# Segment 0 of an attention and Fourier kernel: x turned on the matrix engine, every q and k projected into padded rows, a Fourier token stage in 64-row tiles

## The chip, the cores and the metric

The kernel is one program on one core of a Trainium2 chip. A core has five engines with an instruction stream each: TensorE (PE in the profile, its weight loads PEld), VectorE (DVE), ScalarE (ACT), GpSimd (POOL) and SyncE (SP). SP computes nothing here; it issues nearly all DMAs. Matrix products go to PSUM, eight banks of 128 partitions x 512 f32. The metric is the device time of one execution in microseconds (us).

## The reference

x is 2048 tokens x 640 channels in bf16. Two branches read it, and a gate for each token mixes them.

```python
# branch A: 32 heads of 20 channels, 4 segments of 512 tokens
phi = lambda t: where(t > 0, t + 1, exp(t))
for s in range(4):
    p = softmax(qs @ ks.T * 20**-0.5 + causal_mask)   # inside the segment
    a_dot = p @ vs
    a_mem = (phi(qs) @ M) / (phi(qs) @ z + 1e-6)      # memory of earlier segments
    out[s] = sigmoid(beta) * a_mem + (1 - sigmoid(beta)) * a_dot
    M += phi(ks).T @ vs;  z += phi(ks).sum(tokens)
a = concat(out) @ wo
# branch B: a filter in frequency space, w_r and w_i are 2048 x 321
b = irfft2(rfft2(x) * (w_r + 1j * w_i))
g = sigmoid((x * gate_w).sum(-1));  result = g * a + (1 - g) * b
```

Segment 0 reads no memory, so its q needs no phi; segment 3 updates none, so its k needs none.

## The kernel before

**How the order is set.** Every step is recorded first: a function for each engine that can run it, and the buffers it reads and writes. Which engine takes a step, and the order on each engine, come from one long written list, `ORDER`: each number names an operation and one of its engines. Semaphore waits follow from the buffers. Engines run strictly in their order, so a waiting instruction holds back all behind it on its engine; a DMA that waits on SP holds back the later DMAs on SP. PSUM banks 0 to 3 form one unit, for the scores of four heads at a time; banks 4 to 7 are handed out singly to all other products. PSUM is copied out ("evicted") by ACT (line L523) or DVE (L525).

**Segment 0's start.** Ten matmuls on zeros (`NWARM`) keep PE busy until data arrives. x comes transposed (channels on partitions, tile `xT`) by three transposing DMAs on SP (L546). wq and wk come in two parts, the first 192 columns first.

**q and k.** A head has 20 rows, and a product for the scores wants each head at a partition that is a multiple of 32: the padded tiles `qkp`. For the first two head groups of segment 0 (a group is 4 heads) `proj_direct` (L961) makes these rows on PE directly, four 32-column tiles at a time, which run side by side. All else goes through `proj_tile` (L1027): 128 packed channels per product, evicted to `qu` (for segment 0 to `q0`), stored to DRAM (`qk_scr`, L548) and loaded back with the padding (`pad`, `pad2`, L548). `proj_tile` also makes phi for each 128-channel tile: an exponential on ACT (L1072), a max-add and a min on DVE (L1084, L1085). phi of k then goes through transposing DMAs (`pkT`, L546) into `pkn`, tokens on partitions, for the memory update (`mem_update`, L1334).

**Scores and outputs.** `qk_unit` (L1227) computes the scores of four heads in 12 matmuls of 20 x 64 weights, eight running side by side; ACT takes exp of up to 2048 columns in one instruction (L1263), GpSimd masks the diagonal blocks (L1284). `pv_group` multiplies by v and scales (L1320 to L1330). `mem_read` and `denominators` (L1202 to L1213) build the memory's part: its reciprocals `rc` go to DRAM (`r_scr`) and come back spread over rows (`r`), `finish_tile` (L1506) multiplies (L1526) and adds (L1534), and the output projection (L512) follows.

**Fourier branch** (`fft`, L1365), woven in between. F1 transforms 16 residues of the tokens with the matrix `fcat` (folds at L901, L906); its result goes to `Ac`. For each of 16 groups of token frequencies: D transforms along channels into two tiles `Bt` (real and imaginary); T, four matmuls of 128 x 128 weights and 321 columns, turns tokens and gives two PSUM banks; one DVE product per bank with the filter (`W_mul`, L1439, 642 columns) gives four products `Pt`; two additions on DVE or GpSimd (`W_add`, L1444) give `Yt`; Tb, six matmuls of 256 columns, turns tokens back, into `Cp`. The tables for T and Tb come by DMA (`tt`, 512 KB for two groups), the filter by 32 loads `Wt`. At the end Cp is transformed back along channels and joined with the gate into `G` (L1485).

Of the kernel before, what the change touches and what calls it, by code (L numbers as in the profile page):

```python
# [10 lines left out]
F32 = dt.float32  # L11
# [38 lines left out]
class Sched:  # L50
# [58 lines left out]
    COST = {(0, 1): 94.0, (0, 2): 94.0, (1, 0): 110.0, (1, 2): 110.0, (2, 0): 110.0, (2, 1): 94.0}  # L109

    def schedule(self, pools, order, nsem=56):
# [14 lines left out]
        for i, o in enumerate(pe):  # L126
            o.emode = o.mode
            if o.mode < 0:
                modes = [held[id(b)] for b in o.banks if id(b) in held]
                if not modes and i and pe[i - 1].emode != 1:  # L130
                    modes = [pe[i - 1].emode]
                for q in pe[i + 1:] if not modes else ():
                    m = q.mode if q.mode >= 0 else held.get(id(q.banks[0]), -1)
                    if m >= 0:
                        modes = [0 if m == 1 else m]
                        break
                o.emode = (modes + [0])[0]
            if o.emode != 1:
                for b in o.banks:
                    held[id(b)] = o.emode  # L140
# [167 lines left out]
def make_tables():  # L308
# [42 lines left out]
    T = np.zeros((16, 128, 4, 128))  # L351
    Tp = np.zeros((16, 128, 2, 2, 16, 4, 2))
    n2 = np.arange(16)
    k2 = np.arange(16)
    for g in range(16):
        for half in range(2):
            for i in range(4):
                kb, pi_, kind, sg = pair_of(g, half, i)
                k = kb + 128 * k2
                ph = 2 * pi * np.outer(n2, k) / S  # L360
                c, s = np.cos(ph), np.sin(ph)
                m = half * 64 + k2 * 4 + i
                kr = n2 * 8 + pi_ * 2
                ki = kr + 1

                def put(t, rows, val):
                    T[g, rows[:, None], t, m[None, :]] = val
                if kind == "pair":
                    put(0, kr, c), put(0, ki, sg * s), put(1, kr, -s), put(1, ki, sg * c)
                    put(2, kr, -s), put(2, ki, sg * c), put(3, kr, -c), put(3, ki, -sg * s)  # L370
                else:
                    src = kr if kind == "zero" else ki
                    put(0, src, c), put(1, src, -s), put(2, src, -s), put(3, src, -c)

                def putp(r, typ, eo, val):
                    for q in range(16):
                        Tp[g, m[q], r, typ, :, pi_, eo] = val[:, q]
                if kind == "pair":
                    putp(0, 0, 0, c), putp(1, 0, 0, -s), putp(0, 0, 1, -sg * s), putp(1, 0, 1, -sg * c)
                    putp(0, 1, 0, -s), putp(1, 1, 0, -c), putp(0, 1, 1, -sg * c), putp(1, 1, 1, sg * s)  # L380
                else:
# [1225 lines left out]
```

## Time and profile before

| what | value |
|---|---|
| time, median of 3 runs (lowest, highest) | 243.88 us (243.15, 245.06) |
| span of the profiled execution | 245.4 us |
| instructions | 10243 |
| PE busy | 228.8 us, 93% |
| ACT busy | 199.9 us, 81% |
| DVE busy | 195.6 us, 80% |
| POOL busy | 166.4 us, 68% |
| DMA engines, mean share of queue 1 | 69.2%, 40.96 MB |

The profile is one execution. Its busy table gives each engine's time at work; the slices divide the span into 40 equal parts of 6.1 us and show in tenths how busy each engine was, the clock granted to PE (9 is full) and the share of the DMA engines. Groups of instructions are listed by line and tile with mean times; windows give the same busy times for a chosen stretch. The profiled span lies 1.5 us above the median of the runs, so a change is worked out in microseconds against the span and then taken from the median.

### The profile page before, as it was taken

The page shows a single profiled execution, that of the slowest core. Times are in us where ns is not written, and L with a number is a line of the kernel's source. Part 1 is how long each engine was busy: PE and PEld are TensorE (multiplying, and loading weights), DVE is VectorE, ACT ScalarE, POOL GpSimd, SP SyncE. Part 2 cuts the span into 40 slices and gives each one's busy share as a digit, 9 for nine tenths or more (in the row PEclk, how much of TensorE's full clock was granted, in tenths as well). Part 3 has the DMA queues.
Part 4 walks back from the last instruction along what each step waited for, and adds up shares of the span by engine and source line. Part 5 has one row for each costly group of instructions (what it writes and reads, how often), then busy time and mean ns, then how long its engine had stood idle before and what let it go on. Part 6 is the DMA issues. An engine that isn't in the chain of part 4 may idle for free.

```text
span 245.4 us, 10243 instructions
## 1 busy us (share of the span) xinstructions
PE 228.8 (93%) x4347; PEld 140.8 (57%) x4361; DVE 195.6 (80%) x481; ACT 199.9 (81%) x241; POOL 166.4 (68%) x297
## 2 busy tenths in 40 slices
PE   7899999999999999999899999899999997699994
PEld 2574567765455665545556555465454565366794
DVE  0479998889999987989999898989889867435563
ACT  2289698988999999999899889999999976388740
POOL 8513268557969846768947998859898694359730
PEclk9999999999999999999999999999999999589999
DMA  7999959975799875575698661375758997812123
GB/s 168 278 365 208 239 160 178 318 140 164 210 200 174 168 226 143 125 199 135 202 233 234 185 186 53 99 210 146 222 151 194 230 140 96 127 36 85 57 84 108
DMA packets 58928, 42.17 MB, mean 172 GB/s; under 512 B 30020, under 2 KB 55172, under 8 KB 58884
## 3 DMA queue, kind: packets, MB, share of 16 engines
q1 hardware_dynamic: 57844, 40.96, 69.2%
q8 instruction: 34, 0.56, 1.0%
q10 hardware_dynamic: 1040, 0.57, 0.8%
q14 instruction: 10, 0.08, 0.1%
HBM read 23.32 MB, written 12.30 MB: 145 GB/s over the span
## 4 chain that ended last, share of the span: by engine, by line
PE 54%; DVE 18%; ACT 12%; DMA 10%; issue 3%; SPq 1%; DVEq 0%
PE psum L514 48%; ACT ex L1263 9%; PE psum L512 6%; DMA pkn<-phk 4%; DMA r_scr<-rc 3%; DMA xT<-in_A_x_dram 2%; DVE xsb L906 2%; DVE Pt L1439 2%; DVE xf L901 1%; DVE phk L1085 1%; ACT et L1072 1%; DVE oU L1526 1%; DVE G L1485 1%; DVE ub L525 1%; DVE va L1115 1%
## 5 line engine op out<-in xcount | busy, mean ns | idle before, releaser
L1263 ACT ACTIVATE ex<-psum 128x2048 bf16<-128x2048 f32 (+4 forms) x92 | 138.7, 1507 | 16.3 <-PE psum L514 14.3
L1284 POOL TENSOR_SCALAR_AFFINE_SELECT ex<-ex 128x256 bf16<-128x256 bf16 (+2 forms) x224 | 122.1, 567 | 42.0 <-ACT ex L1263 38.4
L514 PE MATMUL psum<-qkp 20*64 20x64 bf16 (+5 forms) x1280 | 32.7, 271 | 4.8 <-issue 2.3
L514 PE MATMUL psum<-xT,wk 128*128 128x256 bf16 (+1 forms) x280 | 34.0, 273 | 0.9 <-DMA wk<-in_A_wk_dram 0.6
L514 PE MATMUL psum<-wv,xT 128*32 128x321 bf16 (+3 forms) x400 | 30.0, 301 | 0.6 <-DVE va L1115 0.3
L514 PE MATMUL psum<-xT,wq 128*128 128x512 bf16 (+1 forms) x121 | 27.0, 380 | 1.3 <-DMA xT<-in_A_x_dram 0.7
L1439 DVE TENSOR_TENSOR Pt<-psum,Wt 128x642 bf16<-128x642 f32 x32 | 25.5, 820 | 2.3 <-PE psum L514 1.9
L514 PEld LDWEIGHTS psum<-qkp 20*64 20x64 bf16 x1280 | 13.4, 103 | 19.5 <-ACT ex L1263 13.2
L514 PEld LDWEIGHTS psum<-xT,wk 128*128 128x128 bf16 (+1 forms) x280 | 19.9, 97 | 7.0 <-DMA wk<-in_A_wk_dram 1.1
L512 PE MATMUL psum<-wo,oU 128*32 128x320 bf16 x480 | 23.4, 313 | 0.5 <-DVE oU L1534 0.5
L906 POOL TENSOR_TENSOR xsb<-xf 128x320 bf16<-128x320 bf16 (+2 forms) x12 | 9.2, 763 | 17.1 <-DVE xsb L906 13.2
L525 DVE CAST ot<-psum 128x320 bf16<-128x320 f32 x21 | 10.1, 491 | 12.9 <-PE psum L512 10.5
L514 PEld LDWEIGHTS psum<-wv,xT 128*32 128x32 bf16 (+1 forms) x400 | 14.3, 96 | 8.3 <-issue 2.4
L514 PE MATMUL psum<-big,Ac 128*128 128x160 bf16 (+2 forms) x96 | 18.1, 258 | 0.7 <-DVE Pt L1439 0.3
L1115 DVE TENSOR_TENSOR va<-psum,ebx 128x320 bf16<-128x320 f32 x32 | 15.2, 483 | 4.2 <-ACT gate L1113 2.1
L514 PE MATMUL psum<-big,Cp 128*128 128x321 bf16 (+1 forms) x96 | 18.0, 302 | 0.2 <-DVE G L1485 0.2
L514 PE MATMUL psum<-ex,va 128*32 128x64 bf16 (+3 forms) x576 | 17.4, 256 | 0.7 <-DVE dn L1152 0.3
L1485 DVE TENSOR_TENSOR G<-eo,psum 128x320 bf16<-128x320 f32 x32 | 14.7, 482 | 3.9 <-PE psum L514 2.8
L512 PEld LDWEIGHTS psum<-wo,oU 128*32 128x32 bf16 x480 | 12.4, 100 | 8.8 <-issue 4.2
L514 PE MATMUL psum<-tt,Yt 128*128 128x256 bf16 (+1 forms) x96 | 16.5, 275 | 0.3
L514 PEld LDWEIGHTS psum<-ex,va 128*32 128x32 bf16 x576 | 11.1, 96 | 9.7 <-POOL ex L1284 3.4
L1072 ACT ACTIVATE et<-qu 128x512 bf16<-128x512 bf16 x25 | 15.6, 630 | 0.2
(99 smaller groups left out, 391.9 us busy)
## 6 DMA issues: line engine op xcount, KB each, us to landing
qkp<-qk_scr SPq DMA_DIRECT2D x28, 160.0 KB
tt<-tab_tt SPq DMA_DIRECT2D x8, 512.0 KB, 4.3
qk_scr<-qu SPq DMA_DIRECT2D x12, 256.0 KB, 3.1
u_scr<-ub SPq DMA_DIRECT2D x12, 256.0 KB, 3.9
xsb<-in_A_x_dram SPq DMA_DIRECT2D x8, 320.0 KB, 6.8
oU<-u_scr SPq DMA_DIRECT2D x15, 128.0 KB, 2.9
out_dram<-ot SPq DMA_DIRECT2D x12, 160.0 KB
Wt<-in_B_w_r_dram SPq DMA_DIRECT2D x16, 80.2 KB, 2.6
```

Of the source, the lines that this page charges most:

```text
L512: h = e.matmul(dst, wt, r_, start=st, stop=sp_, **{**kw, "tile_position": (0, q), "skip_group_check": True})
L514: h = e.matmul(o_, l_, r_, start=st, stop=sp_, **kw)
L525: alts["dve"] = (lambda e: e.tensor_copy(dst(), src()), 67 + 1.04 * n, 68.0)
L901: self.either(lambda e, r=r, op=op: e.tensor_tensor(xf.ap(r * 642, [321, 2], [1, 320]), xs.ap(o, [D, 2], [1, 320]), xs.ap(o + 320, [D, 2], ...
L906: self.either(lambda e, dst=dst, src=src, d0=d0, n=n, op=op: e.tensor_tensor(xs.ap(o + dst, [D, 2], [1, n]), xf.ap(src + d0, [321, 2], [1, ...
L1072: self.one("act", lambda e: e.activation(et.ap(0, [1, L]), qsl(), ACT.Exp), L, [qb], [b("et", pi_)], late, name="phi_exp")
L1085: fmin = lambda e: e.tensor_tensor(dst(), dst(), et.ap(0, [1, L]), ALU.min)
L1115: self.one("dve", lambda e: e.tensor_tensor(va.ap(i * H * VW + h0 * VW, [VW, nh], [1, DH]), self.ps(bank, 0, [DH, nh], [1, DH]), self.ebx. ...
L1263: self.one("act", lambda e, d=d, q=q: e.activation(self.ex.ap(*d), self.ps(bank, *q), ACT.Exp, scale=SC), n, [bank], [self.exb(s, 2 * pr + ...
L1284: self.one("pool", lambda e: e.affine_select(self.ex.ap(e0 + d0, [1280, 4], [1, n], np_=np_), self.ex.ap(e0 + s0, [1280, 4], [1, n], np_=np_),
L1439: self.one("dve", lambda e, ri=ri, Pt=Pt, Wt=Wt, wo_=wo_, bank=bank: e.tensor_tensor(Pt.ap(ri * 322, [644, 2], [1, KD]), self.ps(bank, 0, ...
L1485: self.one("dve", lambda e, q=q, n2=n2, bank=bank, eo=eo: e.tensor_tensor(self.G.ap(n2 * D + 639 * q, [1 - 2 * q, 320]), eo.ap(q, [1, 320] ...
```

## The change

- **Segment 0's x** is loaded untransposed by two plain DMAs, one on SP and one on ACT's queue, into `xn`, which lies in the third score buffer. `x_turn` turns it on PE: 20 matmuls of 128 columns against the identity in `fcat`, five evictions into `xT`. The zero matmuls go from ten to eight.
- **Segment 0's q and k** all go through `proj_direct`: 16 units instead of 4, each 128 padded rows, straight into `qkp`. The nine packed tiles of segment 0, their stores to DRAM, and the padded loads of segment 0 go.
- **Segment 0's phi of k** comes from `k_tokens`: k is turned token-major on PE (8 banks, 40 matmuls of at most 80 columns), and exp, max and min read or follow these banks, 384 or 256 columns at a time, into `pkn`. Segment 0's three `pkT` transposes go.
- **Fourier token stage**: T's weights are 64 x 128, two row tiles at partitions 0 and 64 with a PSUM bank each (`mode=3`); each bank holds the real and the imaginary part of 64 frequencies. `W_mul` keeps its size and gives `UV`; `W_add` goes, its signs are in Tb's table. Tb has four matmuls of 128 columns per channel block in place of two of 256, writing runs of 4 elements at a stride of 8. The filter is loaded into 64 partitions (36 loads) and copied to the other 64 by 8 DMAs `W_dup` (SP), each waiting for its loads. `tt` is 384 KB.
- **phi of later segments** runs over pairs of tiles: ten instructions of 1024 columns and five of 512 in place of 25 of 512, on each of exp, max and min, with one buffer `et`.
- The gate's transpose runs in 32-column tiles, `rc` lies in `dnc`'s place, and `ORDER` is a new list.

The core of the diff ("..." marks what is left out, all of `ORDER` among it):

```diff
-  NWARM = 10
+  NWARM = 8
...
-  self.xt_load(0, 0.0, 0, 1)
-  self.xt_load(0, 0.01, 1, 2)
-  self.xt_load(0, 0.02, 3, 2)
+  for i in range(2):
+    self.dma(lambda i=i: self.xn.ap(2 * i * D, [D, 2], [1, D]), lambda i=i: dap(x, 2 * i * P * D, [D, P], [P * D, 2], [1, D]),
+        2 * P * D * 2, [], [self.b("xn", i)], 0.0, name="ld_xn")
...
+def x_turn(self):
...
+  for c in range(5):
...
+    bank = Bank(1, "gen", "qk")
+    for i in range(2):
...
+      for q in (2 * i, 2 * i + 1):
+        def th(q=q, c=c, bank=bank):
+          return (self.ps(bank, q * P, [1, P]), self.xn.ap(q * D + c * P, [1, P]), self.fcat.ap(P, [1, P]), True, True, {})
...
+      self.mms(items, [b("xn", i), b("fcat"), bank] + [self.exb(0, 2, k) for k in ("a0", "b0", "b1", "c0", "m1", "m3")], [], -0.9, name="turn", mode=0)
+    self.Sc.op(self.copy_alts(lambda c=c: self.xT[0].ap(c * L, [1, L]), lambda bank=bank: self.ps(bank, 0, [1, L]), L),
...
   else:
-    for n_, (g, which) in enumerate(((0, "q"), (0, "k"), (1, "q"), (1, "k"))):
-      self.proj_direct(which, g, -0.5 + 0.1 * n_, xT, xb)
+    self.x_turn()
+    for n_ in range(16):
+      self.proj_direct("qk"[n_ % 2], n_ // 2, -0.5 + 0.1 * n_, xT, xb)
+    self.k_tokens()
   k = 0
...
+  for half in range(2 if s else 0):
...
-      if s == 0 and half == 0:
...
-          self.dma(lambda j=j, w_=w_, pad=pad: pad.ap((4 * w_ + 2) * L, [L, 2], [1, L], p0=32 * j, np_=DH),
...
-              DH * 2 * L * 2, [b(which + "d", s, half, x) for x in range(2)], [b(which + "p", pidx, j, gl) for gl in (2, 3)], prio, name="pad2")
...
-  pad = self.qkp[0]
+  pad, pidx, gl = self.qkp[g // 4], g // 4, g % 4
+  np_ = 116 if g == 7 else P
+      m = DH if g == 7 and hh == 3 else 32
...
+  self.Sc.op(self.copy_alts(lambda: pad.ap(p0_ + gl * L, [1, L], np_=np_), lambda: self.ps(bank, 0, [1, L], np_=np_), L),
...
+def k_tokens(self):
...
+  for x in range(4):
+    for t0, nt in ((0, 3), (3, 2)):
...
+      bank = Bank(1, "gen")
...
+      for g in range(8):
+        f = max(f0, 80 * g)
+        e_ = min(f1, 80 * g + 80)
...
+        while f < e_:
...
+          def th(g=g, f=f, hh=hh, d=d, n=n, mv=mv, x=x, f0=f0, bank=bank):
+            np_ = 116 if g == 7 else P
+            return (self.ps(bank, f - f0, [1, n]), self.qkp[g // 4].ap((4 + g % 4) * L + x * P, [1, P], np_=np_),
+                self.fcat.ap(P + 32 * hh + d, *mv, np_=np_), True, True, {})
...
+      self.one("act", lambda e, src=src, es=es, m=m: e.activation(self.et.ap(es, [1, m]), src(), ACT.Exp), m, [bank], [eb], 1.0, name="kt_exp")
+      self.one("dve", lambda e, src=src, dst=dst: e.tensor_scalar(dst(), src(), 0.0, 1.0, ALU.max, ALU.add), m, [bank], db, 1.0, name="kt_max")
+      self.Sc.op({"dve": (lambda e, dst=dst, es=es, m=m: e.tensor_tensor(dst(), dst(), self.et.ap(es, [1, m]), ALU.min), 67 + 0.52 * m, 68.0)},
...
+  if t in (1, 2, 4) and ((which == "q" and s >= 1) or (which == "k" and s <= 2)):
+    n = 1 if t == 2 else 2
...
+    et = self.et
-    self.one("act", lambda e: e.activation(et.ap(0, [1, L]), qsl(), ACT.Exp), L, [qb], [b("et", pi_)],
...
+    self.one("act", lambda e: e.activation(et.ap(0, [1, m]), src(), ACT.Exp), m, both, [b("et")], late, after=[b("ets", q) for q in range(2)], fix=94, name="phi_exp")
...
-    self.Sc.op({"dve": (fmax, 67 + 0.26 * L, 68.0)}, r=[qb], w=[db], prio=late, name="phi_max", lock=True, after=alias)
-    self.Sc.op({"dve": (fmin, 67 + 0.52 * L, 68.0)}, r=[b("et", pi_)], w=[db], prio=late, name="phi_min", lock=True)
...
+    self.Sc.op({"dve": (fmax, 67 + 0.26 * m, 68.0)}, r=both, w=db, prio=late, name="phi_max", lock=True)
+    self.Sc.op({"dve": (fmin, 67 + 0.52 * m, 68.0)}, r=[b("et")], w=db, prio=late, name="phi_min", lock=True)
...
-        lambda c=c, nb=nb: self.Ac.ap(c * 2048 + nb * 32, [P, 16], [8, 4], [1, 8]),
...
+        lambda c=c, nb=nb: self.Ac.ap(c * 2048 + nb * 16, [64, 32], [4, 4], [1, 4]),
+        lambda bank=bank: self.ps(bank, 0, [4, 32], [P, 4], [1, 4]), 512),
...
-      self.dma(lambda tt=self.tt[ti]: tt.ap(0, [1024, 2], [1, 1024]), lambda g=g: dap(self.tab["tt"].ap(), g * P * 1024, [1024, P], [P * 1024, 2], [1, 1024]),
...
-          self.dma(lambda r=r, Wt=Wt, h=h, slot=slot, step=step: Wt.ap(r * 644 + slot * KD, [step * KD, 2], [1, KD], p0=64 * h, np_=64),
...
+            self.dma(lambda r=r, Wt=Wt, h=h, o=o, n=n: Wt.ap((4 * r + o) * KD, [KD * 4 // n, n], [1, KD], p0=32 * h, np_=32),
...
+        self.dma(lambda Wt=Wt: Wt.ap(0, [1, 8 * KD], p0=64, np_=64), lambda Wt=Wt: Wt.ap(0, [1, 8 * KD], np_=64), 64 * 8 * KD * 2, wkeys,
+          [b("Wd", wi)], early, name="W_dup")
...
-      self.mms(items, [b("tt", ti), b("Bt", g % 2, 0), b("Bt", g % 2, 1), bank], [], prio2, name="T", mode=0)
-      self.one("dve", lambda e, ri=ri, Pt=Pt, Wt=Wt, wo_=wo_, bank=bank: e.tensor_tensor(
-        Pt.ap(ri * 322, [644, 2], [1, KD]), self.ps(bank, 0, [0, 2], [1, KD]), Wt.ap(wo_, [644, 2], [1, KD]), ALU.mult), 2 * KD,
-        [bank] + wb, [Pb[ri][0], Pb[ri][1]], prio2, after=self.after_q0(("Pt", g % 2, ri)), name="W_mul")
...
-      fn = lambda e, r=r, a0=a0, a1=a1, op=op, Pt=Pt, Yt=Yt: e.tensor_tensor(
-        Yt.ap(r * 322, [1, KD]), Pt.ap(a0 * 322, [1, KD]), Pt.ap(a1 * 322, [1, KD]), op)
-      self.either(fn, KD, [Pb[0][r], Pb[1][1 - r]], [Yb[r]], prio2, after=self.after_q0(("Yt", g % 2, r)), name="W_add")
...
+    UV = self.UV[g % 2]
...
+    pb = [Bank(1, "gen") for _ in range(2)]
...
+    for q in range(2):
+      for rh in range(2):
+        def th(q=q, rh=rh, tt=tt, to=to, Bt=Bt, pb=pb):
+          return (self.ps(pb[rh], 0, [1, KD]), tt.ap(to + q * P, [1, P], p0=64 * rh, np_=64), Bt.ap(q * 322, [1, KD], p0=64 * rh, np_=64),
+              q == 0, q == 1, {"tile_position": (64 * rh, 0)})
...
+    self.mms(items, [b("tt", ti), b("Bt", g % 2, 0), b("Bt", g % 2, 1)] + pb, [], prio2, name="T", mode=3)
+    for rh in range(2):
+      self.one("dve", lambda e, rh=rh, UV=UV, Wt=Wt, gp=gp, bank=pb[rh]: e.tensor_tensor(
+        UV.ap(rh * 644, [322, 2], [1, KD]), self.ps(bank, 0, [0, 2], [1, KD]), Wt.ap((2 * rh + gp) * KD, [4 * KD, 2], [1, KD]), ALU.mult), 2 * KD,
+        [pb[rh]] + wb, [Ub[rh]], prio2, name="W_mul")
...
-            return (self.ps(bank, (c % 2) * 256, [1, 256], np_=kc), Yt.ap(r * 322 + c * P, [1, kc]), tt.ap(to + 512 + r * 256, [1, 256]),
...
-        self.mms(items, Yb + [b("tt", ti), bank], [], prio3, name="Tb", mode=0)
+        for rh in range(2):
+          for w in range(2):
+            def th(c=c, rh=rh, w=w, kc=kc, UV=UV, tt=tt, to=to, bank=bank):
+              return (self.ps(bank, (c % 2) * 256 + rh * 4, [8, 32], [1, 4], np_=kc), UV.ap(rh * 644 + w * 322 + c * P, [1, kc]),
+                  tt.ap(to + 256 + (2 * rh + w) * P, [1, P]), w == 0, w == 1, {"skip_group_check": True})
...
```

## The prediction, on record before the result

> **What bounds the kernel now.** I read the busy table and the slices first, then windows by stage.
>
> ```profile
> PE   7899999999999999999899999899999997699994
> ACT  2289698988999999999899889999999976388740
> DVE  0479998889999987989999898989889867435563
> DMA  7999959975799875575698661375758997812123
> ```
>
> PE is at nine tenths nearly everywhere; ACT and DVE stand at eight or nine until slice 32. No engine is far from full, so an engine that is relieved hands the bound to the next. The windows cut the span at the first exp of the scores (13.30 us) and the first exp of segment 3 (175.50). Columns: stretch, us, busy us of PE, PEld, DVE, ACT, POOL with counts, granted clock, DMA share, GB/s.
>
> ```profile
> 13.00:36.00 23.00, 22.54 (x313) 14.17 (x303) 21.43 (x55) 19.53 (x30) 8.18 (x12) 1.00 0.95 240
> 13.30:175.50 162.20, 156.21 (x2641) 94.71 (x2654) 146.89 (x360) 149.33 (x180) 113.33 (x210) 1.00 0.74 187
> 175.50:245.40 69.90, 62.03 (x1556) 40.62 (x1554) 44.47 (x114) 47.45 (x57) 44.23 (x75) 0.95 0.59 124
> 205.00:209.00 4.00, 3.17 (x108) 2.08 (x106) 3.86 (x12) 2.47 (x4) 1.40 (x1) 1.00 1.00 113
> 211.40:216.20 4.80, 4.79 (x69) 2.43 (x72) 1.39 (x4) 2.74 (x4) 1.50 (x3) 0.50 0.75 117
> ```
>
> In the **middle** (13.30 to 175.50) PE is busy 96.3%, ACT 92.1%, DVE 90.6%. In the **tail** (from 175.50) PE has 7.9 us of gaps, ACT and DVE over 22. Between the last two windows PE stands still for 2.35 us in the middle of a score unit:
>
> ```profile
> 211.41 0.21 PE L514 MATMUL psum<-qkp 20*64 20x64 bf16 x1 [2.35 <-issue]
> ```
>
> "issue" means that nothing in the profile released it: PE had no instruction. One of the 34 instruction fetches (16 KB each, queue 8) was under way while the DMA share was 1.00. Then the clock is halved from 209.4 to 216.2, 6.8 us, which cost about 3.4. Together this **lull** costs 5.75 us.
>
> **The change, part by part.** Prices of PE work come from these rows (start, us, engine, shape, count):
>
> ```profile
> 9.78 1.05 PE L514 MATMUL psum<-xT,wk 128*32 128x256 bf16 x32
> 11.60 1.25 PE L514 MATMUL psum<-xT,wk 128*128 128x256 bf16 x10
> 32.15 0.64 PE L514 MATMUL psum<-fcat,xsb 128*128 128x128 bf16 x8
> 120.41 0.44 PE L514 MATMUL psum<-Bt,tt 128*128 128x321 bf16 x2
> ```
>
> A row lasts one matmul's latency plus a pitch for each further one. Ten matmuls of 256 columns: (1.25 - 0.27) / 9 = 0.109 us. Thirty-two 32-column tiles of 256 columns, four side by side: (1.05 - 0.27) / 7 = 0.111 for four, so a padded unit costs as much as a packed tile, five products of 512 columns, 1.08 us. For 128 columns the pitch is 0.056 to 0.060, for 321 about 0.14.
>
> *PE work.* Segment 0 has 16 padded units in place of 4 units and 9 packed tiles: +3 x 1.08 = +3.3. Turning x: 20 x 0.056 = +1.1. Turning k: 40 matmuls of 80 columns or fewer; at the 128-column pitch 2.4, by columns 1.3; I take 1.3. T: 64 x 0.14 = 9.0 falls to half if the two row tiles run side by side, -4.5; the nearest row is the four 32-column tiles above, which do. Tb: 96 x 0.109 = 10.5 becomes 192 x 0.056 = 10.75, +0.3. Two more switches of tiling than before by the order of instructions, 0.1 each by the gaps at such places, +0.2. Sum **+1.7**, so the change does not relieve PE as a whole. What the trace does not show: whether two row tiles run side by side (bounds -4.5 and 0; no row excludes either), and what Tb's writes in runs of 4 at a stride of 8 cost (no gain, as columns do not fall; at most a doubled pitch, 192 x 0.056 = +10.8). For both I take the nearest rows, whose time follows columns alone.
>
> The Trainium skill ("TensorE: Matmul & The Clock Gate", Measured speedup vs the span model) gives 3.07 times for four row tiles; scaled to two, T would fall by 3.1 instead of 4.5, an estimate, and the forecast would be 1.4 later. No run here shows it yet.
>
> *ACT work.* An exp of 1024 columns takes 1024 ns and one of 512 takes 598, so a pair saves 0.17: 10 pairs of phi, -1.7. Segment 0's phi of k: five of 635 ns become eight of 384 or 256 columns, about 0.49 and 0.38, +0.3. The new list moves evictions (595 ns on ACT, 685 on DVE) to DVE and drops segment 0's: -5 net. Sum **-6 to -7**.
>
> *DVE work.* W_mul stays, 32 of 820 ns. W_add goes: 16 of 370 ns on DVE, -5.9, and 16 of 731 on GpSimd, -11.7. Pairs of phi save about 0.06 on each max and min. The evictions from ACT and the three of x take this back: sum **about 0**. GpSimd takes up other elementwise work, net -6; it is not on the path.
>
> *DMA.* Segment 0 loses three transposing loads of x, 8 stores and 12 padded loads of q and k, and three pkT transposes; one of those stood 4.95 us on the chain of waits (from 71.84). tt moves 1 MB less. Added: four filter loads and 8 copies W_dup, each waiting on SP for its filter loads. Behind a W_dup on SP stand the padded loads and stores of segment 1; SP's waits for filter data are not in the trace of before, and its longest DMA wait (for r_scr) is 3.8 us. Filter loads land in 2.6 us, so a W_dup put right behind them blocks SP at most about that long; where it is put later, nothing. The scores that need those padded loads are released by exps, every 1.9 us, so the cost is 0 to 2.6 for the one that is hit; I take 0, as the next two or three score units are already loaded.
>
> *In time, start.* Before, the first projection waits for x until 5.59 and the first exp starts at 13.31. After, plain loads land like those at the start of the trace: 240 KB issued at 0.80 landed at 4.8, 320 KB issued at 0.79 at 4.1. With 5.3 for both halves of x, 0.3 for the first turns, three evictions on DVE (2.05), the 3.9 of projection that then remain ahead of the first scores and 0.55 for these, the first exp starts at 12.1: **-1.1**. Bounds: -2 if x lands at 4.4; +0.5 if PE idles between the eight zero matmuls and x and the clock halves.
>
> *In time, middle.* I counted the work that stands ahead of segment 3's first exp in both orders, with the trace's mean times: PE -2.3, ACT -6.8, DVE -2. The Fourier groups are spread later, so PE's share moves behind that point. The stretch can shrink by no less than PE's 2.3 if its 6 us of gaps stay, and by ACT's 6.8 if ACT paces it. "ACT ex waits for PE" sums to 14.3 us in 29 waits and "PE waits for ex" to 13.2 in 42: they pace each other about equally, so I take the middle: **-4.5**.
>
> *In time, tail.* PE has 3.8 us more behind that exp and 7.9 us of gaps, 2.35 of them the lull. Bounds 0 and +3.8, half taken: **+1.9**. The lull I leave as it is: the same kind of burst (transposes of the outputs, tables) meets the same code.
>
> Sum: -1.1 - 4.5 + 1.9 = -3.7. Against the profiled execution 245.4 - 3.7 = 241.7; it lay 1.5 above the median, so **243.88 - 3.7 = 240.2**. A change within 1% (241.4 to 246.3) can hardly be told from none by these runs.
>
> **Rivals.**
>
> 1. *The lull goes.* Thirty-three of 34 fetches stop nobody; one falls into a full DMA window. All transfers shift, so it may simply miss: 240.2 - 5.75 = **234.4**.
>
> 2. *DVE holds the middle.* DVE is busy 90.6% there, W_mul is not shorter, and evictions are moved to it. If it takes ACT's place the middle gains nothing: 243.88 - 1.1 + 1.9 = **244.7**, no change. Against it: ACT gives up work that DVE takes only as W_add goes. The Trainium skill ("TensorEngine Tiling (Array Packing)", PSUM Bottleneck) warns of this: tiling speeds up TensorE, but not the emptying of PSUM. The rows agree that W_mul's share stays; by this rule T's saving would be worth nothing in the middle.
>
> 3. *PE runs out of instructions in segment 0* (slower). The 16 padded units are 480 matmuls and 480 weight loads in 17 us of PE time, 55 instructions per us; in 205 to 209, ahead of the lull, it was (108 + 106) / 4 = 53, and the DMA share was 1.00 there and is 0.95 in 13 to 36. From 210 to 232 PE ran as fast at a share of 0.38 without a stop. So both conditions meet in the new segment 0, unless the DMAs that go (the q, k round trip) empty the queues. Each stall costs up to 5.75: one gives 245.9, two **251.7**; it decides from the second on.
>
> 4. *The change doesn't do what it says*: row tiles one after the other give 240.2 + 4.5 = 244.7, Tb at twice its pitch 240.2 + 10.8 = **251**.
>
> **How the numbers follow.** Forecast 0.44, with its own range 237.2 to 243.2 (middle and tail at their bounds, start aside); lull gone 0.20; DVE 0.17; instruction supply 0.13; not as said 0.06. Faster by over 1%: three quarters of the forecast 0.33, the lull 0.20, DVE 0.01, together 0.54. Within 1%: 0.11 + 0.11 + 0.03 = 0.25. Slower: DVE 0.05, supply 0.10, not as said 0.06, together 0.21. The range is 234 to 249: it leaves out about half of the lull's case below and the dearest cases above.
>
> **What the profile after would show.** Right: the first exp near 12.1; T's row with four matmuls of 321 columns in the time of two; no L1444 and 32 W_mul of some 820 ns; ACT's sum down by 6; the first exp of segment 3 near 170. Wrong: the filter product waiting behind evictions with DVE over 95% busy; "issue" waits above 1 us before 30 us and a clock of 0.5 after them; Tb's 128-column rows at 0.1 apart; SP waiting for filter loads while PE waits for qkp. What would upset the forecast most is a lull that goes, comes twice, or comes elsewhere.

## The result, and the profile after

| | median of runs, us (lowest to highest) | profiled execution: span, time | ratio to before |
|---|---|---|---|
| before, beside it | 244.47 (243.15 to 246.54, 4 runs) | 245.4, – | 1 |
| after | 256.99 (253.21 to 259.4, 4 runs) | 256.6, 258.44 | 1.045, 95% interval 1.034 to 1.056 |

The change costs about 4.5%; the ratio is taken over the faster executions of each kernel, the medians over all four, and the profiled execution of after (258.44) is one of the slower two of its four. I had forecast 240.2 in a range of 234 to 249: wrong in sign and outside the range.

The slices of the changed kernel, 40 of 6.4 us, in tenths; PEclk is the granted clock of PE:

```profile
PE   5886999899999999999999999989999999999993
DVE  0434689988898999988899984988999897987462
ACT  1154688758999999998889989988898887677410
PEclk9799799979999999999999999999999999999999
DMA  7999300326338595886797676895599666557224
```

From slice 5 on PE is about as full as before, but slices 2 to 4 have 8, 8 and 6, and the clock is below full in slices 2, 5 and 9. The dip in slices 36 and 37 of before (the lull) is gone. The windows say the same (stretch, us, busy us of PE, PEld, DVE, ACT, POOL with counts, granted clock, DMA share, GB/s); the first exp is at 15.70 and segment 3's first at 184.20:

```profile
13.00:36.00 23.00, 19.67 (x520) 12.62 (x512) 12.00 (x28) 14.28 (x18) 8.26 (x13) 0.93 0.67 188
15.70:184.20 168.50, 158.59 (x3030) 97.15 (x3023) 143.29 (x309) 143.83 (x162) 105.73 (x201) 0.98 0.63 154
184.20:256.60 72.40, 64.85 (x1603) 43.85 (x1600) 55.50 (x141) 47.83 (x61) 47.67 (x78) 1.00 0.61 143
25.00:28.00 3.00, 3.00 (x51) 1.31 (x46) 1.17 (x3) 1.87 (x1) 0.77 (x1) 0.50 0.89 266
52.00:56.00 4.00, 4.00 (x79) 2.34 (x72) 3.38 (x7) 2.21 (x3) 2.40 (x5) 0.57 0.06 15
```

ACT and DVE are less busy ahead of segment 3 than they were (ACT 143.8 for 149.3, DVE 143.3 for 146.9; PE, partly at half its clock, 158.6 for 156.2), and yet the middle is 168.5 us for 162.2. The tail is 72.4 for 69.9, though the old one held the lull; DVE's busy time there rose from 44.5 to 55.5. PE's rows at the places where it stood (start, us, engine, shape, count, in brackets the idle time before it and what ended it):

```profile
7.66 1.67 PE L517 MATMUL psum<-fcat,xn 128*128 128x128 bf16 x16 [2.66 <-DMA xn<-in_A_x_dram]
18.27 1.60 PE L517 MATMUL psum<-xT,wk 128*32 128x256 bf16 x50 [1.27 <-issue]
24.57 0.29 PE L517 MATMUL psum<-xT,wk 128*32 128x256 bf16 x3 [2.06 <-issue]
50.80 0.46 PE L517 MATMUL psum<-wv,xT 128*32 128x320 bf16 x8 [1.21 <-DVE va L1148]
```

The first is the late second half of x. The next two are rival 3: PE had no instruction, in the padded units of segment 0, and after the second the clock is 0.50 (25 to 28). Ahead of them PE took (150 + 142) / 4.5 = 65 and (91 + 80) / 2.9 = 59 instructions per us, with the queues full (0.99 and 1.32):

```profile
12.50:17.00 4.50, 4.50 (x150) 3.41 (x142) 2.23 (x5) 2.89 (x4) 1.71 (x4) 1.00 0.99 330
19.50:22.40 2.90, 2.90 (x91) 1.84 (x80) 1.99 (x5) 2.49 (x3) 0.77 (x1) 1.00 1.32 243
```

A 16 KB fetch of queue 8 shows at 15.66 and at 22.22; PE goes on 2.6 and 2.4 us after it. Ahead of the lull of before it was the same: fetch at 208.76, PE at 211.41.

To place the loss I cut each profiled span at the starts of the 92 exps of the scores (the 61st is segment 3's first; "again" is the changed kernel run once more, e8, and "512" the kernel of the first experiment; in brackets before without its lull):

| stretch, us | before | after | again | 512 | 512, second time |
|---|---|---|---|---|---|
| start to 1st exp | 13.3 | 15.7 | 12.5 | 12.8 | 12.9 |
| 1st to 9th | 36.3 | 41.5 | 39.2 | 34.7 | 34.7 |
| 9th to 49th | 100.1 | 97.3 | 97.3 | 97.7 | 97.9 |
| 49th to 61st | 25.8 | 29.7 | 28.9 | 29.3 | 31.2 |
| 61st to 92nd | 57.1 (52.4) | 56.4 | 60.0 | 57.9 | 57.8 |
| behind the 92nd | 12.8 | 16.0 | 15.7 | 14.9 | 15.0 |
| span | 245.4 (240.7) | 256.6 | 253.6 | 247.3 | 249.5 |

Two losses can be read off. The first is in the start and segment 0: +7.6 for after, of which 3.2 (x late) did not come again and 2.3 more go mostly with the clock, at half for 3.4 us behind a stop in after and not in e8; the same kernel again loses 2.1 there, and the 512 kernel gains 2.1. The second begins at the 49th exp and is in all four.

The span without the lull is the right thing to compare with. The lull cost less than the 5.75 us I gave it: the clock was at half from 209.4 to 216.2, but PE stood until 211.41, and half a clock costs nothing while PE stands. That leaves 2.35 + (216.2 - 211.41) / 2 = 4.75, and a span of 240.7, which is also the median span of the other 21 executions of before whose spans were kept. A run's time is its span and 1.7 to 2.1 us; by this the profiled execution of before would have taken some 247, and the other executions of before took 241 to 245 (25 runs in four groups, group medians 242.3 to 244.5; two runs lay above, at 246.5 and 248.4). The lull was a mishap of that one execution.

### The profile page after: what moved, and what is told of

The parts are those of the page before. It is cut to its first block, busy times and chain, and to the rows that moved or that the text cites. A ratio compares the mean times of both kernels' runs of the same rounds, so it can differ in the third digit from the quotient of the medians.

```text
span 256.6 us, 11076 instructions
## 1 busy us (share of the span) xinstructions
PE 235.2 (92%) x4805; PEld 147.7 (58%) x4805; DVE 203.2 (79%) x457; ACT 195.7 (76%) x227; POOL 160.8 (63%) x290
## 4 chain that ended last, share of the span: by engine, by line
PE 59%; DVE 20%; DMA 12%; issue 3%; ACT 2%; SPq 2%; ACTq 0%; DVEq 0%
PE psum L517 55%; PE psum L515 4%; DMA Wt<-Wt 3%; DVE UV L1479 3%; DMA oU<-u_scr 3%; DMA xn<-in_A_x_dram 2%; DMA Wt<-in_B_w_i_dram 2%; DVE G L1521 2%; ACT ex L1296 2%; SPq L551 2%; DVE ub L528 1%; DVE oU L1562 1%; DMA Wt<-in_B_w_r_dram 1%; DVE phq L1117 1%; DMA r_scr<-rc 1%
## 5 line engine op out<-in xcount | busy, mean ns | idle before, releaser
L517 PE MATMUL psum<-xT,wk 128*32 128x256 bf16 (+1 forms) x470 | 35.9, 281 | 3.6 <-issue 3.3
L517 PE MATMUL psum<-xT,wq 128*32 128x512 bf16 (+1 forms) x235 | 36.4, 413 | 0.1
L517 PE MATMUL psum<-wv,xT 128*32 128x320 bf16 (+3 forms) x400 | 32.1, 308 | 1.6 <-DVE va L1148 1.4
L1479 DVE TENSOR_TENSOR UV<-psum,Wt 128x642 bf16<-128x642 f32 x32 | 25.3, 821 | 4.3 <-PE psum L517 2.2
L517 PEld LDWEIGHTS psum<-xT,wk 128*32 128x32 bf16 (+1 forms) x470 | 21.6, 101 | 11.4 <-issue 6.3
L517 PEld LDWEIGHTS psum<-wv,xT 128*32 128x32 bf16 (+1 forms) x400 | 14.9, 97 | 10.8 <-issue 2.9
L915 POOL TENSOR_TENSOR xsb<-xf 128x322 bf16<-128x322 bf16 (+2 forms) x13 | 9.8, 756 | 18.0 <-DVE xf L910 13.5
L1148 DVE TENSOR_TENSOR va<-psum,ebx 128x320 bf16<-128x320 f32 x32 | 14.9, 481 | 4.2 <-PE psum L517 3.5
L517 PE MATMUL psum<-big,Ac 128*128 128x321 bf16 (+2 forms) x96 | 16.8, 257 | 0.2 <-DVE va L1148 0.2
L517 PE MATMUL psum<-tt,UV 128*128 128x128 bf16 (+1 forms) x192 | 16.5, 221 | 0.3
L517 PEld LDWEIGHTS psum<-xT,wq 128*32 128x32 bf16 (+1 forms) x235 | 10.8, 101 | 8.5 <-issue 1.7
L528 DVE CAST qu<-psum 128x512 bf16<-128x512 f32 x21 | 14.3, 683 | 1.6 <-PE psum L517 0.9
```

Of the source, the lines that this page charges most:

```text
L517: h = e.matmul(o_, l_, r_, start=st, stop=sp_, **kw)
L528: alts["dve"] = (lambda e: e.tensor_copy(dst(), src()), 67 + 1.04 * n, 68.0)
L915: self.either(lambda e, dst=dst, src=src, d0=d0, n=n, op=op: e.tensor_tensor(xs.ap(o + dst, [D, 2], [1, n]), xf.ap(src + d0, [321, 2], [1, ...
L1148: self.one("dve", lambda e: e.tensor_tensor(va.ap(i * H * VW + h0 * VW, [VW, nh], [1, DH]), self.ps(bank, 0, [DH, nh], [1, DH]), self.ebx. ...
L1479: self.one("dve", lambda e, rh=rh, UV=UV, Wt=Wt, gp=gp, bank=pb[rh]: e.tensor_tensor(UV.ap(rh * 644, [322, 2], [1, KD]), self.ps(bank, 0, ...
```

## The experiments

**What was to be told apart.** S: PE runs out of instructions where segment 0's k is projected in products of 256 columns. Its rivals: the late x of the start; the length of the middle, by one engine or another; more work behind segment 3's first exp. All kernels are the changed one with the edit shown, unless said otherwise. Runs of before beside them: median 242.26 for the first four, 242.71 for the next four, 243.15 for the last four (7 runs each).

### Segment 0's k in products of 512 columns (e1_k512)

Before and after, k of segment 0 is projected in the token order of its tile, for which a product is cut into two of 256 columns. Here the product is whole and the eviction reorders: 160 pairs of weight load and matmul fewer, the same columns.

```diff
-  for o, n, src in self.token_order(which, xT, c):
+  for o, n, src in ((0, L, lambda c=c: xT.ap(c * L, [1, L])),):
...
+  def turned(e, put):
+    put(e, pad.ap(p0_ + gl * L, [128, 2], [1, 128], np_=np_), self.ps(bank, 0, [256, 2], [1, 128], np_=np_))
+    return put(e, pad.ap(p0_ + gl * L + 256, [128, 2], [64, 2], [1, 64], np_=np_), self.ps(bank, 192, [256, 2], [-64, 2], [1, 64], np_=np_))
```

> The changed kernel, but k of segment 0 is projected in products of 512 columns in place of two of 256 (160 matmul and load pairs fewer), and the copy out of PSUM puts the tokens in order with two instructions. Column work and DMAs are as before. In the changed kernel TensorE stood without instructions for 1.27 us at 17.0 and 2.06 us at 22.5, and its clock was halved from 25 to 28.3. Theory S (TensorE uses up its instructions, at 55 per us, faster than a fetch comes while the DMA queues are full): at some 37 per us both stops are gone or under 0.5 us, the time falls by 3 to 5 us, to about 252 to 254. Rival Q (the full queues alone delay a fetch, whatever the rate): stops of more than 1 us stay, at other places, the time falls by less than 2. Rival P (these stops are hidden by later slack): the stops go and the time stays within 1 us of 257.

Measured: 249.95 us (247.24 to 255.65), ratio 1.029 (1.021 to 1.037). Its window beside that of after above, and the row of the place where after stopped:

```profile
13.00:36.00 23.00, 22.89 (x417) 12.54 (x408) 18.66 (x48) 19.42 (x30) 13.03 (x20) 1.00 0.69 189
12.62 2.77 PE L517 MATMUL psum<-xT,wk 128*32 128x512 bf16 x48
```

PE is busy 22.89 us of 23 where it was 19.67, at 36 instructions per us, at the same DMA share (0.69 for 0.67) and a full clock. The fetches still come (13.18, 18.48), and stop nobody. Nor are the queues emptier where the fetches fall; from 6 to 26 us they are full:

```profile
6.00:26.00 20.00, 20.00 (x404) 9.74 (x406) 14.16 (x33) 14.32 (x23) 8.38 (x13) 1.00 1.10 318
```

That is 40 instructions per us for 20 us at a share of 1.10, and PE is never idle: full queues alone (rival Q) don't stop it. S holds. It is worth 4.5 us (against the changed kernel again) to 6.7 (against after) between the 1st and 9th exp; the medians, with all else that differed between executions, differ by about 6.3 (the two of after against the two of this kernel, 256.8 and 250.5). What remains, some 3%, is not S.

### SP held back (e2_hold), the start's transfers held back (e3_start), both the start and 512 (e4_both)

Does S need full DMA queues? In e2 an early entry of SP's list, and all behind it, waits for the tenth padded unit's eviction. In e3 SP's third transfer waits for the first turning product, so that x comes alone. e4 is e3's edit and 512 columns.

```diff
+  HOLD = [('sp', 10, 'ev_projd', 9)]   # e2;  ('sp', 2, 'turn', 0) in e3 and e4
+  for e_, i_, name_, j_ in self.HOLD:
+    o_, p_ = queue[e_][i_], [q for q in ops if q.name == name_][j_]
+    o_.preds.append(p_); p_.succs.append(o_)
```

> The changed kernel, but SyncE's transfers from the head mask on (mask, beta, x quarters, segment 1's x, the large table, the first filter and token tables) wait for the eviction of the tenth padded unit of segment 0, so that the DMA queues are empty while most of segment 0 is projected. The instruction rate is unchanged. Theory S and rival Q: no stop without instructions over 0.5 us between 16 and 25 us, exps 1 to 3 earlier by 3 to 5 us; some of it may be given back where segment 1's x comes later, 252 to 256 in all. If the rate alone were the cause (a fetch cannot keep up with 55 per us even on empty queues): the stops stay, 257 or more.

> The changed kernel, but SyncE's third transfer and all behind it wait for the first turning matmul, so that the two halves of segment 0's x and the first weights have the DMA engines for themselves. In the changed kernel the second half landed at 7.6 us, the clock was halved from 8 to 11.4 and the first exp began at 15.7. Theory: the halves land by about 5.5, the clock stays full, the first exp begins at 12 to 13, the time falls by 2.5 to 3.5 us. Rival: the first exp comes earlier, but segment 0 then waits for the rest of the weights or runs into the same instruction stops, and the time falls by less than 1.

> The 512-column k of the first experiment and the held start of the third together. If both causes add: 6 to 8.5 us under the changed kernel, 248 to 251. If one of them only uncovers the other: no more than 5 us.

| | us | ratio | first exp | stops without instructions |
|---|---|---|---|---|
| e2 | 255.25 | 1.0535 (1.048 to 1.059) | 12.6 | 1.42 ahead of 15.36, none at 16 to 23.9, then one of 0.65 |
| e3 | 254.07 | 1.046 (1.037 to 1.054) | 13.0 | 1.56 ahead of 15.89, 1.79 ahead of 21.91 |
| e4 | 251.14 | 1.0285 (1.018 to 1.039) | 12.5 | none above 0.6 |

PE in e2, first its two stops, then the stretch with SP held back:

```profile
15.36 1.60 PE L523 MATMUL psum<-xT,wk 128*32 128x256 bf16 x50 [1.42 <-issue]
24.83 0.38 PE L523 MATMUL psum<-xT,wk 128*20 128x256 bf16 x5 [0.65 <-issue]
16.00:24.00 8.00, 8.00 (x239) 5.24 (x232) 5.54 (x12) 5.88 (x8) 2.67 (x4) 1.00 0.41 106
```

In the held stretch PE took (239 + 232) / 8 = 59 instructions per us for 8 us without a stop, at a DMA share of 0.41. Both stops stand where the queues are full (the share was 1.02 from 13 to 15 and 2.01 from 23.9 to 25). So S takes both a high rate and full queues, as rival 3 said. But e2 is hardly faster than after: from the 9th to the 49th exp it takes 99.2 us for 97.3, which fits that what SP was kept from loading came late, but no run separates it. e3 and e4 show that the start alone is worth little: with x on time the first exp is at 12.5 to 13.0, and in e3 the stops remain. Its median is 2.7 below after's 256.8, about what I had expected, but its profiled span (253.9) is that of the changed kernel again (253.6), where x came in time without any hold. e4 is not below the 512 kernel, and at 5.7 below after it lies between my two marks.

### The old kernel with segment 0's products cut in four (e5_split)

The kernel before, with segment 0's q and k products in 128 columns: 310 pairs more, the same columns, nothing else of the change.

```diff
+  if split and which == "q":
+    return [(o, P, lambda o=o: xT.ap(c * L + o, [1, P])) for o in range(0, L, P)]
+  if split:
+    return ([(o, P, lambda o=o: xT.ap(c * L + 2 * o, [1, P])) for o in (0, P)] + ...
```

> The kernel before, with one edit: every product of segment 0's q and k is cut into pieces of 128 columns (four for 512, two for 256), the same columns and results with about 310 more matmul and load pairs, and no DMA changed. Its DMA share from 13 to 34 us is 0.99. Theory S (instructions run out where the rate passes some 50 per us while the DMA queues are full): TensorE now stops without instructions for more than 1 us at least once between 8 and 30 us, and the time rises by 2 to 7 us. Rival (the stops of the changed kernel come from its own DMAs or from the padded products, not from the rate): no such stop, the time within 1.5 us of the kernel before.

Measured: 252.6 us (251.35 to 252.66), ratio 1.038 (1.033 to 1.044). PE's longest waits, its rows and two windows:

```profile
PE psum L514 <- issue: 6.9, 5, 5.6
9.66 0.28 PE L514 MATMUL psum<-xT,wk 128*32 128x128 bf16 x5
15.51 1.79 PE L514 MATMUL psum<-xT,wk 128*32 128x128 bf16 x59 [5.58 <-issue]
9.50:15.50 6.00, 0.43 (x29) 0.26 (x17) 0.00 (x0) 0.00 (x0) 1.48 (x2) 0.87 1.04 366
15.50:20.50 5.00, 4.99 (x126) 4.79 (x127) 2.82 (x7) 1.68 (x3) 0.94 (x1) 0.50 1.03 254
```

At (149 + 141) / 2.1 = 138 instructions per us (7.8 to 9.9, share 0.89) PE comes to one stop of 5.6 us with the queues full (1.04), then runs at half the clock. The first exp is 8.0 us late (21.3), and the 73rd is still 7.8 late: nothing downstream gives a delay back. This shows S by itself, without any of the change's other parts. (In its profiled tail a stop of 0.87 us stands in place of the lull's 2.35; from the 61st exp on it takes 67.3 us.)

### The Fourier part alone in the old order (e6_fourier)

The kernel before, with only the new Fourier token stage; the order is the old one, with 58 instructions moved to fit it, most by one place (shortened; the comments are added here).

```diff
-  name="T", mode=0)     # four 128 x 128, W_mul with 2 x 642, W_add
+  name="T", mode=3)     # two row tiles of 64, W_mul into UV, Tb in runs of 4
+  self.dma(... Wt.ap(0, [1, 8 * KD], p0=64, np_=64), ... Wt.ap(0, [1, 8 * KD], np_=64) ..., name="W_dup")   # right behind its loads
```

> The kernel before, with the Fourier part of the change alone: 64-row tiles, UV in place of Pt and Yt, the new tables, filter loads and copies. The old order is kept but for what this part forces (additions gone, the copies right behind the filter loads, 58 instructions moved, most by one place). Segment 0 and phi stay as they were. TensorE loses about 4 us of work, DVE 6, GpSimd 12. Theory 1 (TensorE bounds, this part gains, segment 0's part and the order lose): 2 to 5 us under the kernel before. Theory 2 (the wait for the copied filter, or two PSUM banks held at once, takes it back): within 1.5 us of it or slower.

Measured: 277.8 us, ratio 1.141 (1.134 to 1.148). The waits:

```profile
PE psum L517 <- DVE UV L1446: 16.3, 12, 5.9
DVE UV L1446 <- DMA Wt<-Wt: 14.7, 3, 7.7
DVE UV L1446 <- PE psum L517: 13.1, 11, 4.9
```

DVE's filter product waits 14.7 us for the copied filter, and PE as long for it; besides, the clock is at half for 30.7 us in all. This does not price T and Tb, as I had meant it to: in the old order no part can be told apart beside these waits. In the changed kernel's own order `W_mul` waited 1.8 us for copies.

### Less work in the tail (e7_nodb), the changed kernel once more (e8_again)

e7 is the 512 kernel without the third of three terms in the last Fourier product, 32 matmuls; it leaves out the last 65 channel frequencies. e8 has no edit.

```diff
-  for c in range(3):
-    kc = 65 if c == 2 else P
+  for c in range(2):
+    kc = P
...
-  big.ap(1288 + (typ * 3 + c) * 322, [1, KD], np_=kc), c == 0, c == 2, {})
+  big.ap(1288 + (typ * 3 + c) * 322, [1, KD], np_=kc), c == 0, c == 1, {})
```

> The 512-column k of the first experiment, and the third of the three terms in each of the 32 products of the last Fourier stage left out (32 matmuls, 4.8 us of TensorE, all behind segment 3's first exp; the filter's result lacks its last 65 channel frequencies). Theory 1 (TensorE's work bounds the tail): 3.5 to 5.5 us under the first experiment. Theory 2 (the tail waits for the chain of memory reciprocals, DVE or the transfers): less than 2 us under it.

> The changed kernel once more, on the chip of these runs, to see which of its stops return. Theory S: the two stops without instructions at 16.7 and 22.2 us return within 3 us of these places, since rate and queues are the same; the late second half of x (7.6 us) does not, as two kernels with the same first transfers had it at 5.0. Ratio to the kernel before 1.04 to 1.055.

e7: 251.1 us, ratio 1.031 (1.023 to 1.039), not faster than 512 by its runs. In the profiles the stretch from the 61st exp to the end is 69.4 for 72.8, so 3.4 of the 4.8 us taken from PE, but its first exp was 1.8 late. By its runs that is my theory 2 (less than 2 us to gain), by its profile nearly theory 1. Profiles of the changed kernels differ by up to 4.4 us in this very stretch (71.3 to 75.7), so e7 settles neither.

e8: 256.59 us (253.39 to 260.21) beside 242.71; the medians give 1.057. The stops recur, at nearly the same products (its PE rows):

```profile
15.47 1.60 PE L517 MATMUL psum<-xT,wk 128*32 128x256 bf16 x50 [1.63 <-issue]
21.48 0.29 PE L517 MATMUL psum<-xT,wk 128*32 128x256 bf16 x3 [1.79 <-issue]
```

while x's second half was on time and the first exp at 12.5. So the late x varies from execution to execution, and the stops are systematic. In this profile another wait shows, in the tail:

```profile
203.30 0.99 PE L517 MATMUL psum<-big,Cp 128*128 128x321 bf16 x3 [2.40 <-DVE on L1358]
```

Six of the eleven profiles with the new order have it, at 2.3 to 2.4 us (e2, e3, e4, e8, e11, e13), with half the clock behind it, and none with the old order; those six take 73.3 to 75.7 us from the 61st exp on, the four others with the same work there 71.3 to 72.9.

### One engine's work lengthened in the middle (e11_pe, e12_act, e13_dve), with 512 again (e14_k512)

By then I thought PE alone paced the middle (P), since ACT's relief had brought nothing. Each kernel is the 512 kernel with 3 to 6 us more for one engine.

```diff
+  twice = [((lambda th=th: th()[:4] + (True,) + th()[5:]), n) for th, n in items[:2]]   # e11: T
+  items = twice + twice + items
...
+  for o in range(0, m, pw):          # e12: phi_exp; pw is 128, 512, 256 for t = 1, 2, 4
+    h = e.activation(et.ap(o, [1, pw]), qt.ap(qo - (n - 1) * L + o, [1, pw]), ACT.Exp)
...
+  for o in range(0, m, pw):          # e13: phi_min
+    h = e.tensor_tensor(ph.ap(po + o, [1, pw]), ph.ap(po + o, [1, pw]), et.ap(o, [1, pw]), ALU.min)
```

> The kernel with segment 0's k in products of 512 columns, and the first two of each group's four T products made three times (64 matmuls more, two side by side, about 0.14 us a pair: PE +4.5 us, all between the first exp and segment 3's first exp). Theory P, PE alone sets the pace of the middle: the stretch between these two exps grows by 4 to 4.5 over the same kernel without the repeats. Rival A, the one of my prediction, that ACT and PE pace the middle about equally: it grows by about half, 2.3. Rival D, DVE holds it: 0 to 1.

> The same kernel with the ten phi exps of 1024 columns cut on ACT into eight of 128 (five of them) or four of 256 columns (the other five): 50 instructions more, at a fixed cost of 0.06 to 0.17 us each ACT +3 to +8.6 us, all between the first exp and segment 3's first. Theory P: the stretch between these two exps grows by at most 1. Rival A: by half of what ACT's busy time grows by, 1.5 to 4.3. Rival D: 0 to 1.

> The same kernel with the ten min instructions of phi of 1024 columns cut on DVE in the same way: 50 instructions more, at 0.06 to 0.16 us each DVE +3 to +8 us in the same stretch. Theory P and rival A: the stretch grows by at most 1. Rival D, DVE holds the middle: by most of what DVE's busy time grows by, 3 to 8.

> The kernel with segment 0's k in products of 512 columns once more, beside the three that lengthen one engine's work: 161.7 us between its first exp and segment 3's first, within 1, by every theory; and no stop without instructions above 0.5 us before 30 us.

Times: 253.42, 251.9, 255.67 and 251.13 us; ratios 1.041 (1.032 to 1.050), 1.036 (1.030 to 1.042), 1.052 (1.045 to 1.058), 1.034 (1.029 to 1.040). The last agrees with the first 512 kernel in all but one stretch: T waited 2.0 us for its table `tt` in 49th to 61st (0.9 the first time), so that 1st to 61st is 163.8 and not 161.7 within 1. I compare up to the 53rd exp, ahead of that wait. Windows, in the order e14, e11, e12, e13:

```profile
12.87:156.40 143.53, 136.46 (x2558) 81.95 (x2564) 127.47 (x281) 127.37 (x144) 97.24 (x183) 1.00 0.69 165
```

```profile
15.32:161.50 146.18, 139.54 (x2606) 84.33 (x2612) 127.69 (x281) 127.47 (x145) 97.31 (x183) 1.00 0.66 158
```

```profile
13.00:159.40 146.40, 137.23 (x2558) 81.98 (x2564) 127.68 (x281) 131.17 (x192) 97.89 (x183) 1.00 0.67 163
```

```profile
14.24:162.00 147.76, 136.79 (x2558) 82.14 (x2564) 133.22 (x328) 127.48 (x145) 96.88 (x183) 1.00 0.65 158
```

PE +3.1 busy: the stretch +2.65. ACT +3.8: +2.9. DVE +5.75: +4.2. Every engine's added work is paid at 0.74 to 0.86 of its length. This is one profile each, but the four kernels with nothing added in the middle (both 512 ones, e4, e7) lie within 143.3 to 143.9. In this stretch P falls, and so do the other two theories: no single engine paces it, nor two in equal parts. I read it as a chain: work on PE, ACT and DVE follows in turn in one written order, and an addition stands in the way wherever it is made. The times of whole runs say less. The medians lie 2.3 (PE), 0.8 (ACT) and 4.5 us (DVE) over the 512 kernel beside them, and only DVE's range stands clear; alone they would also fit rival D. In its profile the kernel with more ACT work had made up the loss by the end (span 249.7 for 249.5).

## Why the prediction was wrong, by its steps

Three steps failed: the supply of instructions stood in the sum at nothing, the middle's −4.5 took PE and ACT to share the pace and looked at no part of the stretch by itself, and the tail's +1.9 was too small. The start's −1.1 and the base failed by less.

**Instruction supply (rival 3): the mechanism right, the chance wrong.** Both conditions were named, and both met; I gave it 0.13 because the transfers that go might empty the queues. They did not: the share was 0.87 at 16 to 19 and 1.00 at 22 to 25. The price, up to 5.75 a stop, was too high: 1.3 and 2.1 us of standing and some 1.6 of half clock after the second, in all 4.5 to 6.7 between the 1st and 9th exp for both. (The window 210 to 232 of before, which I called free of a stop, holds the last 1.4 us of the lull's.) The Trainium skill ("Runtime: NRT & Kernel Launch", Instruction fetch mechanics) has the sequencer fetch blocks of 16 KiB ahead and calls the cost mostly hidden. The runs agree on the block and, at 40 instructions per us with full queues, on the hiding; at 53 to 138 with full queues there were stops of 1.3 to 5.6 us.

**Middle, −4.5: right up to the 49th exp, wrong from there.** From the 1st to the 49th exp the 512 kernel takes 132.4 us for 136.4, −4.0; after would have it without its stops (9th to 49th, −2.8). Then it is given back: the 49th to the 61st takes 29.3 for 25.8. I had counted the work up to the 61st exp as one sum, and not what stands in its last part. There now stand 84 matmuls of Tb (before 28, twice as wide) and 99 of v's projection (before 50), and T waits there for `tt`, 0.9 to 2.0 us. The first filter product starts at 82.3 in after, 73.3 in 512 and 53.9 before: the Fourier groups are late from the outset, and their queue has to be worked off ahead of the last products. That this work makes up the +3.5 is argued from the counts; no run took it out. From the 1st to the 61st exp 512 thus has −0.5 and +1.7 in its two profiles where I had −4.5, the changed kernel again +3.2. After has +6.3: it has the stops, and half the clock (0.57 from 52 to 56) behind a 1.21 us wait for `va`; all kernels with the new order have this wait, most of them with a full clock behind it.

**ACT −6 to −7: right in kind, its worth misjudged.** ACT's busy time fell by 5.5 in the middle (4.2 in all). Taking the midpoint between PE's −2.3 and ACT's −6.8 assumed that two engines share the pace, and I read that from two sums of waits (14.3 and 13.2) that don't show it: they are of the whole span, and the second is idle time of the weight loads, not of PE. In the middle of before, ACT and PE themselves waited for each other like this (us, times, longest):

```profile
ACT ex L1263 <- PE psum L514: 5.7, 16, 0.9
PE psum L514 <- ACT ex L1263: 1.5, 6, 0.4
```

The last three profiles fit a chain through three engines, in which added work costs nearly its length. Whether relief in it, without a tighter order around it, brings as much is shown by no run.

**Tail, +1.9: mis-sized; about +7.7.** In 512 the stretch from the 61st exp on is 72.8, against 69.9 with and 65.2 without the lull; over all profiles with the same work there it is 71.3 to 75.7, so +6 to +10.5. PE's work behind that exp is not +3.8 but about +6: all 96 matmuls of the last Fourier product (before, 32 of them were ahead of it), at some 0.15 each 4.8, and 12 more of `Mz`. And nothing is absorbed where I took half: the stretch grows by more than PE's work does. Behind the last exp are 120 matmuls of weights by v (`va,ex`) for 70, and that stretch is 2.1 longer. "DVE about 0" failed, too: +7.6 us in all (203.2 for 195.6), and in the tail 55.5 busy for 44.5. One part of this is one multiplication that takes longer, `oU<-oU,mT` (min, median, max in ns; first before, then after):

```profile
L1534 DVE TENSOR_TENSOR oU<-oU,mT x7: 428/484/1078, 195.6 to 225.7; 128x640 bf16<-128x640 bf16 x7
```

```profile
L1570 DVE TENSOR_TENSOR oU<-oU,mT x8: 492/828/1532, 210.3 to 233.8; 128x640 bf16<-128x640 bf16 x8
```

In after those of 492 and 493 lay beside 0.18 and 0.16 us of GpSimd's masks, those of 943 and 1532 beside 0.6 and 1.6. The Trainium skill ("SBUF — State Buffer", Terms) says that VectorE and GpSimd share a port pair, which one holds while the other waits. The rows of after fit that, and so does the one ahead of the 2.40 us wait of e8, where a product `oU<-oU,r` took 2.25 us beside masks back to back (another in this profile took 0.36); but two of before's `oU<-oU,mT` ran in 428 and 484 ns beside GpSimd all along, so the runs do not settle it.

**Start, −1.1** (by its own terms 13.3 - 12.1 = 1.2)**.** The first exp was at 15.7, and at 12.5 in the same kernel run again; so −0.8 when x is in time and +2.4 when its second half lands at 7.6 and PE idles until its clock is at half (0.51 from 9.2 to 11.4). My upper bound of +0.5 named this case, but took it that x lands by 5.3.

**The base.** I took the forecast from the median, which has no lull, and left the lull in both kernels as it was. That execution's time, some 247, was therefore about 3.3 above the median (I had set its span against the median, 1.5), and rival 1, "the lull goes", with a chance of 0.20, had nothing to win. The forecast's own range, too, was narrower than its terms: with middle and tail at their bounds it is 236.0 to 244.3, not 237.2 to 243.2.

**Right.** Two row tiles do run side by side: four matmuls of 321 columns take 0.45 us where two took 0.44, and T's times from start to start sum to 6.8 us (7.2 in 512) for 10.9, −3.7 to −4.1 where I had −4.5. That is 34 to 38% of T. The Trainium skill's factor ("TensorE: Matmul & The Clock Gate", Measured speedup vs the span model), scaled to two tiles, had given 34%, an estimate, and I had chosen 50%: the rule was closer. Tb did not double: 12.9 for 13.7. Turning k took 1.5 for 1.3. `W_mul` stayed. A row of after, and its group:

```profile
81.63 0.45 PE L517 MATMUL psum<-Bt,tt 64*128 64x321 bf16 x4
...
L1479 DVE TENSOR_TENSOR UV<-psum,Wt 128x642 bf16<-128x642 f32 x32 | 25.3, 821 | 4.3 <-PE psum L517 2.2
```

The copied filter (0 taken) was cheap in this order: DVE waited 1.8 us for it.

Summed up in time: 13 us from before's 243.6 to after's 256.8 (means of the two medians each, from the two groups that have after). The supply of instructions in segment 0 is 4.5 to 6.5 of it, shown by 512, e2 and e5. What is left is in the new order, and all kernels with it have it: in spans, 512 gains 4.5 up to the 49th exp against before without its lull and loses some 11 behind it, 6.6 in all. No run undid that loss, so its cause stays in part open. What a better order for the same parts would give stays open too: no version here beats the kernel before, and the best is the 512 kernel at 1.029 to 1.034.

## What to carry to other kernels

Count PE's instructions per microsecond, not only its columns, wherever the DMA queues are full: at 53 and more, here, PE ran dry, at 40 over 20 us it did not (where the limit lies between them no run tells), and wider products of the same columns cured it. Compare a change with the median of several executions stage by stage, and take a mishap that one profile shows out of the base first. In a chain of interlocked engines, count the work that stands behind each point in the new order, and not one sum for a long stretch: a lead of 4 us at the 49th exp was gone by the 61st.

## What the runs showed of the hardware that I had not expected

- PE resumed 2.4 to 2.7 us after its 16 KB fetch showed in the queue (15.66 to 18.27, 22.22 to 24.57 in after, 208.76 to 211.41 before, 13.12 to 15.51 in the split kernel), though the fetch itself took 1.0 to 1.2.
- With the DMA share at 0.41, PE took 59 instructions per us for 8 us without a stop.
- The same wait can cost the clock or not: a wait of 1.15 to 1.21 us for `va` stands in all eleven profiles with the new order, and the clock then went to half for 3.4 us in two (after, e3) and stayed full in nine. At the start it went to half after a wait of 2.66 us for x (after) and stayed full after one of 2.10 (e11).
- PSUM writes in runs of 4 elements at a stride of 8 cost nothing that shows (Tb 12.9 us for 13.7, 13.1 in 512).
